# Moving the decode of the second MoE's weights out of the x2 stages, with three result buffers and two raw weight buffers

## The chip, the cores and the metric

The kernel runs on one core of a Trainium2 chip. Its metric is the device time of one execution in microseconds (us), and the median of several executions is what is compared. The engines are named as the profile names them: PE (TensorE, with its weight loads as PEld), DVE (VectorE), ACT (ScalarE), POOL (GpSimd), SP (the queue that issues nearly all DMAs here).

## The reference

An attention with packed queries, a first MoE and a second MoE, one after the other. There are 8 batches, 8 heads, 576 positions, 64 columns a head, so 4608 tokens of 512 columns.

```python
p_packed = sm_attn(p, k, v)            # 32 packed queries for each head
x = sm_attn(q, p_packed, p_packed)     # 576 queries on 32 keys
x = x.transpose(0, 2, 1, 3).reshape(4608, 512)
y = maximum(maximum(x @ w1, x @ w2), x @ w3)   # 512 -> 768
x2 = y @ w_out                                 # 768 -> 512
h = x2 @ w_in                                  # 512 -> 2048
P = a[0] + a[1]*h + a[2]*h**2 + a[3]*h**3
Q = 1 + abs(b[0])*abs(h) + abs(b[1])*h**2
out = (P / (Q + 1e-6)) @ w_out2                # 2048 -> 512
```

All weights of the two MoEs arrive as 64-bit floats.

## The kernel before

**Arithmetic.** Every fp32 product is made of three matmuls of a high and a low part (`mm3`, lines 61 to 63). A weight in 64 bits has to be taken apart into these parts on the core first. `decode` (lines 76 to 95) does it for one piece of 128 rows: it loads the raw words (`w_raw`, 64 bits a number), and then runs five instructions on DVE (L76, L80 or L78, L85, L87, L92 or one of them less), two on ACT (L81, L82) and one on POOL (L95). All DVE instructions of it read or write `w_raw`.

**Stages.** The first MoE goes over four pairs of batches (`bp` 0 to 3). For each pair there is a stretch of y stages: six blocks `f` of the 768 columns, two batches and three weights `w1`, `w2`, `w3` each, so 36 turns of 12 matmuls, and behind each turn the function `between` puts other work in. The maximum over the three weights is kept in a tile `hm` of the pool `hx`. The attention is folded into the weights: `m_stage` (L313) multiplies a tile of weights `wt` by the packed attention into the matrix `m` that y uses, twelve times a pair. Behind the y stages come eight x2 stages (`x2_stage`, two batches by four blocks of 128 columns), which multiply the maxima by `w_out`, bring the result from PSUM into a tile `hm` again (L477, on ACT or DVE) and store it to memory (L478). Between the x2 stages of pairs 0 to 2 stands the second softmax of the next pair (`s2_stage`, lines 275 to 293), whose transposed result also takes a tile `hm` (L293). PSUM has two banks pairs, `psy`, for y, x2 and this softmax.

**The two feeds.** `feed` decodes the first MoE's 12 pieces of w1 to w3 and 4 pieces of w_out during pair 0 (pieces of 768 columns). `feed2` decodes the second MoE's 32 pieces (512 columns) during pairs 1 to 3. One `feed2.step()` finishes a piece (L85, L87, L92 and POOL's L95 write it into a tile `wt`), stores it to memory (L235), issues the load of a further raw piece (L100) and starts the next piece (L76, L80, ACT's L81 and L82). The first step only starts one. Before the change the steps stand behind turns 1, 5, ..., 33 of the y stages of pairs 1 and 2, behind four x2 stages of pair 1 and three of pair 2, and behind turns 1, 5, ..., 29 of pair 3: 13 + 12 + 8 = 33 steps.

**Rings.** `wt` is a ring of four tiles that the decoded pieces share with the `w1` to `w3` tiles, which are read back from memory for each pair (`again`, L216). A `wt` tile that `m_stage` has used is free for the next that waits. `w_raw` is a ring of three, and `feed` and `feed2` load that many pieces ahead. `hm` is a ring of two.

**What sets the order.** The program's order is not that of the queues. The framework simulates the program at build time and issues, of the instructions whose inputs and buffers are there, the one that stands earliest in the program; a buffer that comes free goes to the earliest of those that wait. So decoding can be pulled ahead of the turn where it is written, as far as the rings allow. On the chip each engine keeps the order found in that way and waits for what is late. The second MoE's matrix work (`h_mm`, `g_stage`, `o_mm`) begins when the last x2 stage is done and runs to the end.

Of the kernel before, what the change touches and what calls it, by code (L numbers as in the profile page):

```python
# [33 lines left out]
def attn_moe_moe2_kernel(  # L34
# [16 lines left out]
    def split(hi, lo, src, hi_eng="act", lo_eng="dve"):  # L51

        if hi_eng == "act":
            act.copy(hi, src)  # L54
        else:
            nc.vector.tensor_copy(hi, src)
        e = dve if lo_eng == "dve" else pool
        e.tensor_tensor(out=lo, in0=src, in1=hi.bitcast(F32), op=ALU.subtract)  # L58
# [108 lines left out]
    bstack, ctx2 = ExitStack(), ExitStack()  # L167
# [10 lines left out]
    rstack = ExitStack()  # L178
    wp = rstack.enter_context(tc.tile_pool(name="wp", bufs=1, side="right"))
    mp = [rstack.enter_context(tc.tile_pool(name=f"mp{x}", bufs=1, side="right")) for x in range(2)]  # L180
    hx = bstack.enter_context(tc.tile_pool(name="hx", bufs=2))


    wt_ready, NWT, NW = {}, 4, 12
# [16 lines left out]
        return tiles, w123[2 * f + g], keep, True  # L201

    used = itertools.count()
    NRAW = 3

    def next_wt():

# [16 lines left out]
    def w2_pieces():  # L224

        for i in range(32):
            box = []

            def tiles(box=box):
                box.append(wt_tile())  # L230
                hi, lo = (box[0][:, x] for x in range(2))
                return (hi.bitcast(I32) if wide else hi.bitcast(F32R)), lo.bitcast(F32R)

            def keep(box=box, i=i):
                nc.sync.dma_start(w2_scr[:, :, 512 * i : 512 * i + 512], box[0])  # L235

            yield tiles, w_2[i], keep, False

    def load_w2(tiles, o, n):

        for x in range(2):
            nc.sync.dma_start(tiles[:, x].bitcast(F32), w2_scr[:, x, 512 * o : 512 * (o + n)])
# [56 lines left out]
    def m_tiles(f):  # L299

        return [mp[f % 2].tile([128, 2, 2, 384], F32R, name=f"m{x}") for x in "hl"]

    def m_stage(bp, g, mt):

        ps = ps_t.tile([128, 2, 512], F32, name="pst")
        wt, n = next_wt()
        for b2 in range(2):
            for h in range(4):  # L310
                i, j = divmod(h, 2)
                l, c = slice(64 * j, 64 * j + 64), 32 * (h ^ b2)
                pe.matmul(ps[c : c + 32, b2, :384], lhsT=ppk[l, bp % 2, 2 * g + b2, 32 * h : 32 * h + 32],  # L313
                          rhs=wt[l, 384 * i : 384 * i + 384], start=True, stop=True)
        again(n)
        split(*(t[:, :, g, :] for t in mt), ps[:, :, :384])
# [130 lines left out]
    def y_stage(b2, f, m, a2, between, lo_eng):  # L447
        hm = hx.tile([128, 2, 288], F32, name="hm")
        mh, ml = m
        for w in range(3):  # L450
            ps = ps_y.tile([128, 2, 512], F32, name="psy")
            for half in range(2):
                for g in range(2):
                    ah, al = a2[g]
                    c = slice(288 * half, 288 * half + 288)
                    mm3(ps[:, half, :288], mh[:, g, 128 * w : 128 * w + 128], ml[:, g, 128 * w : 128 * w + 128],
                        ah[:, c], al[:, c], g == 0, g == 1)
            if w == 0:
              act.copy(hm, ps[:, :, :288])
            else:  # L460
              dve.tensor_tensor(out=hm, in0=ps[:, :, :288], in1=hm, op=ALU.max)  # L461
            between()
        hh = hp_pool.tile([128, S], F32R, name=f"hh{b2}{f}")
        hl = hp_pool.tile([128, S], F32R, name=f"hl{b2}{f}")
        split(hh, hl, hm.rearrange("p a b -> p (a b)"), lo_eng=lo_eng)
        return hh, hl
# [13 lines left out]
    def wi_at(f):  # L480

        if f < 1:
            return wi_0
        return wi_b[:, :, f - 1]
# [18 lines left out]
    ahead = Ahead(0)  # L503
    feed = Feed(wp, pieces, NRAW)
    for x in "P L0 L1 W0 R W1 L2 L3 R".split():
# [5 lines left out]
    pool.memset(cln[:, 1:2], -LN64)  # L511
    feed2 = None

    y_steps = {1: range(1, 36, 4), 2: range(1, 36, 4), 3: range(1, 32, 4)}
    windows = (), (0, 2, 4, 6), (1, 3, 5)
    for bp in range(NBP):
        turn = itertools.count()
        if bp == 1:
            feed2 = Feed(wp, w2_pieces(), NRAW, NRAW)
        if bp == NBP - 1:  # L520

            nc.sync.dma_start(av, a_in.partition_broadcast(128))
            nc.sync.dma_start(bv, b_in.partition_broadcast(128))
            dve.tensor_scalar(out=babs, in0=bv, scalar1=-1.0, scalar2=None, op0=ALU.mult)
            dve.tensor_tensor(out=babs, in0=babs, in1=bv, op=ALU.max)
        now = ahead
        a2, mt = ahead.a2, ahead.mt
        hs = [[None] * 6, [None] * 6]
        if bp + 1 < NBP:
            ahead = Ahead(bp + 1)  # L530
            for x in "P L0 W0 L1 W1".split():
                ahead.do(x)
            pack = ahead.steps(PACK)
        else:
            pack = iter(())
        for f in range(6):
            if f < 5:
                nmt = m_tiles(f + 1)

            def between(bp=bp, f=f, now=now):  # L540
                t = next(turn)
                if now.soft:
                    now.do("g")
                if f < 5 and t % 6 in (2, 4):
                    m_stage(bp, t % 6 // 2 - 1, nmt)
                if t >= 2:
                    next(pack, None)
                if bp == 0:
                    if t % 3 < 2 and t < 32:
                        feed.half_step()  # L550
                elif t in y_steps[bp]:
                    feed2.step()

            if bp == NBP - 1 and f == 2:
                load_w2(wi_at(0), 0, 1)
            for b2 in range(2):
                hs[b2][f] = y_stage(b2, f, [t[:, b2] for t in mt], a2[b2], between,
                                    "dve" if bp == 0 or (b2, f) == (1, 5) else "pool")
            mt = nmt
        if bp + 1 < NBP:  # L560
            assert not list(pack)
            gen = ahead.steps(SECOND)
            for m in range(4):
                for b2 in range(2):
                    x2_stage(2 * bp + b2, m, hs[b2])
                    next(gen, None)
                    if bp == 0:
                        feed.half_step()
                    if 2 * m + b2 in windows[bp]:
                        feed2.step()  # L570
            if bp == 0:
                assert not feed.raw and not feed.half
            next(gen, None)
            assert not ahead.soft
        else:
            assert not feed2.raw and not feed2.half
            rstack.close()
            NQA = 1
            wr = ctx.enter_context(tc.tile_pool(name="wr", bufs=1, side="right"))
            xpa = ctx.enter_context(tc.tile_pool(name="xpa", bufs=1, side="right"))  # L580
            wi_b = wr.tile([128, 2, 15, 512], F32R, name="wi_b")
            wq_a = wr.tile([128, 2, NQA, DM], F32R, name="wq_a")

            def wq_at(f):
                return wq_a[:, :, f] if f < NQA else wq_b[:, :, f - NQA]

            def load_x(blk, xp):
                xh = xp.tile([128, 4, 512], F32R, name="xh")
                xl = xp.tile([128, 4, 512], F32R, name="xl")
                for kc in range(4):  # L590
                    xr = xp.tile([128, 512], F32, name="xr", bufs=1)
                    nc.sync.dma_start(xr, x2_scr[:, kc, 512 * blk : 512 * blk + 512])
                    split(xh[:, kc, :], xl[:, kc, :], xr, lo_eng="pool" if blk > 1 else "dve")
                return xh, xl

            loads = [(wi_at(f), f) for f in range(1, 16)] + [(wq_at(f), 16 + f) for f in range(NQA)]
            per = -(-len(loads) // 8)
            for b2 in range(2):
                for m in range(4):
                    for _ in range(min(per, len(loads))):  # L600
                        tiles, o = loads.pop(0)
                        load_w2(tiles, o, 1)
                    if (b2, m) == (0, 2):
                        xc = load_x(0, xpa)
                    x2_stage(2 * bp + b2, m, hs[b2])
# [129 lines left out]
```

## Time and profile before

| | |
|---|---|
| time, median of 3 runs (lowest to highest) | 1390.62 us (1390.1 to 1392.14) |
| time of the profiled execution | 1393.72 us |
| its span, first to last instruction | 1391.8 us |
| mean granted clock of PE in it | 0.975 |
| PE busy | 1313.8 us, 94% of the span |
| DVE busy | 1051.1 us, 76% |
| ACT busy | 802.2 us, 58% |
| POOL busy | 242.7 us, 17% |

The time of an execution holds some 2 us outside the span. Busy shares are means over stages with different limits, so the stages are looked at one by one further on. A granted clock of 1 is 2.4 GHz, one of 0.5 is 1.2 GHz.

### The profile page before, as it was taken

How to read it: one execution, taken by the hardware profiler on the slowest of the kernel's cores; microseconds unless marked ns; L12 is line 12 of the kernel's file. 1: busy time of each engine (PE TensorE's matmuls, PEld its weight loads, DVE VectorE, ACT ScalarE, POOL GpSimd, SP SyncE). 2: the span in 40 equal slices, each digit the busy share in tenths (PEclk: the TensorE clock that was granted, in tenths of full speed). 3: DMA queues.
4: the chain of work that ended last, by engine and by line, in shares of the span. 5: the costliest groups of instructions: out<-in, count | busy, mean ns of one | idle time of the engine just before them, and what ended most of it. 6: DMA issues, size and time to landing. Idle time of an engine off the chain costs nothing.

```text
span 1391.8 us, 21572 instructions
## 1 busy us (share of the span) xinstructions
PE 1313.8 (94%) x8496; PEld 1091.5 (78%) x8496; DVE 1051.1 (76%) x1630; ACT 802.2 (58%) x1337; POOL 242.7 (17%) x230
## 2 busy tenths in 40 slices
PE   4479899998999899999999999999999999999998
PEld 1267788878878789978888888888888888888886
DVE  5877845767677765178888988888888888888887
ACT  3444523543443333176766867768677686776765
POOL 3542242425333533000100101001010010100000
PEclk9589899999999999999999999999999999999999
DMA  9945544677464721970100101001001010010000
GB/s 307 308 138 167 158 144 145 213 230 245 155 209 156 237 93 55 325 278 1 47 14 1 61 1 38 23 0 62 0 25 37 0 54 0 16 38 1 31 0 31
DMA packets 51557, 140.86 MB, mean 101 GB/s; under 512 B 5632, under 2 KB 5632, under 8 KB 50688
## 3 DMA queue, kind: packets, MB, share of 16 engines
q1 hardware_dynamic: 51168, 138.96, 30.0%
q8 instruction: 67, 1.10, 0.3%
q10 hardware_dynamic: 288, 0.52, 0.1%
q14 instruction: 34, 0.28, 0.1%
HBM read 99.09 MB, written 40.37 MB: 100 GB/s over the span
## 4 chain that ended last, share of the span: by engine, by line
PE 81%; DVE 5%; DMA 4%; ACT 2%; issue 1%; POOL 1%; SPq 0%; ACTq 0%; POOLq 0%; DVEq 0%
PE po L61 10%; PE po L62 9%; PE po L63 9%; PE psh L62 9%; PE psh L61 9%; PE psh L63 9%; PE psy L61 8%; PE psy L62 7%; PE psy L63 7%; PE pst L313 2%; DMA wi_b<-w_scr 1%; DMA w_raw<-in_w_dram 1%; DMA x_scr<-hm 1%; PE pst L378 1%; DVE wt L87 1%
## 5 line engine op out<-in xcount | busy, mean ns | idle before, releaser
L61 PE MATMUL po<-wq_b,gh 128*128 128x512 f32 x540 | 212.3, 393 | 0.8 <-ACT gh L54 0.8
L62 PE MATMUL po<-wq_b,gh 128*128 128x512 f32 x540 | 211.3, 391 | 0.0
L62 PE MATMUL psh<-xl,wi_b 128*128 128x512 f32 x540 | 211.0, 391 | 0.0
L63 PE MATMUL psh<-xh,wi_b 128*128 128x512 f32 x540 | 210.6, 390 | 0.0
L61 PE MATMUL psh<-xh,wi_b 128*128 128x512 f32 x540 | 210.6, 390 | 0.0
L634 ACT ACTIVATE hb<-psh,babs 128x512 f32<-128x512 f32 (+1 forms) x145 | 100.2, 691 | 188.8 <-PE psh L63 188.8
L61 PE MATMUL psy<-a2h,mh 128*128 128x288 f32 x576 | 181.6, 316 | 17.1 <-DVE hm L461 8.1
L63 PE MATMUL po<-wq_b,gl 128*128 128x512 f32 x540 | 181.7, 391 | 0.0
L637 DVE SCALAR_TENSOR_TENSOR hb<-h,babs,hb 128x512 f32<-128x512 f32 (+1 forms) x145 | 108.2, 746 | 97.1 <-ACT h L635 97.0
L62 PE MATMUL psy<-a2l,mh 128*128 128x288 f32 x576 | 172.7, 300 | 4.4 <-POOL a2l L58 4.4
L63 PE MATMUL psy<-a2h,ml 128*128 128x288 f32 x576 | 172.0, 299 | 0.0
L58 POOL TENSOR_TENSOR xl<-xr,xh 128x512 fp32r<-128x512 f32 x28 | 36.6, 1306 | 633.5 <-ACT xh L54 633.5
L61 PEld LDWEIGHTS psy<-a2h,mh 128*128 128x128 f32 x576 | 110.3, 192 | 44.4 <-issue 12.9
L61 PE MATMUL psy<-hh,wo_h 128*128 128x288 f32 x384 | 117.2, 305 | 12.1 <-ACT hm L477 11.7
L63 PEld LDWEIGHTS po<-wq_b,gl 128*128 128x128 f32 x540 | 101.3, 188 | 24.0
L461 DVE TENSOR_TENSOR hm<-psy,hm 128x576 f32<-128x576 f32 x96 | 72.4, 754 | 63.2 <-PE psy L63 60.3
L61 PEld LDWEIGHTS po<-wq_b,gh 128*128 128x128 f32 x540 | 101.4, 188 | 22.9 <-ACT gh L54 1.2
L62 PEld LDWEIGHTS po<-wq_b,gh 128*128 128x128 f32 x540 | 101.4, 188 | 22.4
L61 PEld LDWEIGHTS psh<-xh,wi_b 128*128 128x128 f32 x540 | 101.4, 188 | 22.1
L62 PEld LDWEIGHTS psh<-xl,wi_b 128*128 128x128 f32 x540 | 101.4, 188 | 21.7
L63 PEld LDWEIGHTS psh<-xh,wi_b 128*128 128x128 f32 x540 | 101.4, 188 | 21.7
L62 PE MATMUL psy<-hl,wo_h 128*128 128x288 f32 x384 | 115.5, 301 | 0.0
(104 smaller groups left out, 2816.0 us busy)
## 6 DMA issues: line engine op xcount, KB each, us to landing
w_raw<-in_w_dram SPq DMA_DIRECT2D x32, 512.0 KB, 4.7
w_scr<-wt SPq DMA_DIRECT2D x32, 512.0 KB, 3.3
wt<-w_scr SPq DMA_DIRECT2D x36, 384.0 KB, 4.0
kt<-in_k_dram SPq DMA_DIRECT2D x16, 576.0 KB, 6.2
vraw<-in_v_dram SPq DMA_DIRECT2D x16, 576.0 KB, 6.5
w_raw<-in_w_dram SPq DMA_DIRECT2D x12, 768.0 KB, 12.0
kt<-in_q_dram SPq DMA_DIRECT2D x16, 576.0 KB, 6.2
x_scr<-hm SPq DMA_DIRECT2D x32, 288.0 KB, 3.3
```

Source lines behind the costliest of these rows:

```text
L58: e.tensor_tensor(out=lo, in0=src, in1=hi.bitcast(F32), op=ALU.subtract)
L61: pe.matmul(out_ap, lhsT=lh, rhs=rh, start=first, stop=False)
L62: pe.matmul(out_ap, lhsT=lh, rhs=rl, start=False, stop=False)
L63: pe.matmul(out_ap, lhsT=ll, rhs=rh, start=False, stop=last)
L87: dve.scalar_tensor_tensor(out=hib, in0=hw, scalar=-0x80000000, in1=t, op0=ALU.bitwise_and, op1=ALU.bitwise_or)
L313: pe.matmul(ps[c : c + 32, b2, :384], lhsT=ppk[l, bp % 2, 2 * g + b2, 32 * h : 32 * h + 32], rhs=wt[l, 384 * i : 384 * i + 384], start=Tru ...
L378: pe.matmul(pv[32 * h : 32 * h + 32, :64], lhsT=at[:, 3 * i + cp, o : o + 32], rhs=vt[:, h, c, :], start=c == 0, stop=c == VC - 1)
L461: dve.tensor_tensor(out=hm, in0=ps[:, :, :288], in1=hm, op=ALU.max)
L634: act.activation(hb, h, AF.Abs, scale=babs[:, 0:1])
L637: dve.scalar_tensor_tensor(out=hb, in0=h2, scalar=babs[:, 1:2], in1=hb, op0=ALU.mult, op1=ALU.add)
```

## The change

Four edits. The pool `hx` gets three buffers instead of two. `NRAW`, the number of `w_raw` buffers and of raw pieces loaded ahead, becomes two instead of three; it holds for both feeds, so for the start of the kernel too. The steps of `feed2` between the x2 stages are gone, and the y stages have more: behind turns 1, 4, ..., 34 in pairs 1 and 2, and behind 1, 5, ..., 33 in pair 3. The count is 12 + 12 + 9 = 33 again.

```diff
-    hx = bstack.enter_context(tc.tile_pool(name="hx", bufs=2))
+    hx = bstack.enter_context(tc.tile_pool(name="hx", bufs=3))
...
-    NRAW = 3
+    NRAW = 2
...
-    y_steps = {1: range(1, 36, 4), 2: range(1, 36, 4), 3: range(1, 32, 4)}
-    windows = (), (0, 2, 4, 6), (1, 3, 5)
+    y_steps = {1: range(1, 36, 3), 2: range(1, 36, 3), 3: range(1, 36, 4)}
...
                     if bp == 0:
                         feed.half_step()
-                    if 2 * m + b2 in windows[bp]:
-                        feed2.step()
```

## Rows read from the trace of the kernel before

**Rows 1.** The page's chain that ended last, share of the span by engine.
```profile
PE 81%; DVE 5%; DMA 4%; ACT 2%; issue 1%; POOL 1%; SPq 0%; ACTq 0%; POOLq 0%; DVEq 0%
```

**Rows 2.** Windows: length, PE, PEld, DVE, ACT, POOL busy (instructions), clock, DMA share, GB/s.
```profile
0.00:54.00 54.00, 25.72 (x381) 12.29 (x381) 31.87 (x63) 20.96 (x40) 19.95 (x34) 0.81 0.98 316
54.00:172.20 118.20, 94.36 (x919) 74.29 (x919) 95.67 (x136) 57.27 (x93) 38.98 (x36) 0.86 0.53 170
172.20:215.90 43.70, 43.30 (x381) 39.86 (x377) 18.91 (x33) 11.21 (x18) 14.92 (x12) 1.00 0.38 130
215.90:298.70 82.80, 80.51 (x892) 66.92 (x890) 53.76 (x93) 38.25 (x71) 29.79 (x34) 1.00 0.60 188
298.70:350.50 51.80, 46.39 (x379) 42.91 (x373) 37.92 (x64) 18.59 (x30) 24.77 (x18) 0.93 0.75 255
350.50:434.00 83.50, 80.51 (x890) 66.89 (x888) 54.81 (x93) 38.18 (x71) 29.51 (x34) 1.00 0.50 163
434.00:487.60 53.60, 47.27 (x411) 42.81 (x405) 41.95 (x69) 20.44 (x32) 25.89 (x19) 0.94 0.72 237
487.60:554.40 66.80, 65.21 (x529) 58.76 (x528) 38.29 (x53) 24.58 (x38) 22.31 (x16) 1.00 0.21 72
554.40:592.80 38.40, 38.38 (x290) 38.15 (x288) 5.73 (x8) 7.52 (x13) 0.00 (x0) 1.00 0.90 314
594.90:1391.80 796.90, 792.10 (x3456) 648.67 (x3456) 670.86 (x1019) 564.59 (x934) 36.56 (x28) 1.00 0.09 32
```

**Rows 3.** Waits in 298.7:350.5: total us, times, longest.
```profile
PE psy L61 <- ACT hm L477: 5.4, 3, 2.4
```

**Rows 4.** Waits in 434:487.6.
```profile
PE psy L61 <- ACT hm L477: 6.3, 2, 5.3
```

**Rows 5.** Timeline around one such wait: start us, duration us, instruction [idle before, releaser].
```profile
320.07 1.60 POOL L283 TENSOR_TENSOR e<-e,mx 128x576 f32<-128x576 f32 x1
...
320.58 1.38 DVE L80 TENSOR_SCALAR dec_r<-w_raw 128x512 int32<-128x512 int32 x1
...
321.99 0.63 ACT L82 ACTIVATE dec_r<-dec_r 128x512 f32<-128x512 int32 x1 [3.39 <-DVE dec_r L80]
...
322.52 0.62 ACT L477 COPY hm<-psy 128x576 f32<-128x576 f32 x1
```

**Rows 6.** Windows of instructions on w_raw: length, DVE, POOL busy (instructions), clock, DMA, GB/s.
```profile
54.00:172.20 118.20, 46.26 (x49) 7.85 (x4) 0.86 0.53 170
172.20:215.90 43.70, 0.00 (x0) 0.00 (x0) 1.00 0.38 130
215.90:298.70 82.80, 20.07 (x35) 9.65 (x7) 1.00 0.60 188
298.70:350.50 51.80, 22.66 (x31) 7.85 (x6) 0.93 0.75 255
350.50:434.00 83.50, 20.97 (x35) 9.39 (x7) 1.00 0.50 163
434.00:487.60 53.60, 26.01 (x36) 9.16 (x7) 0.94 0.72 237
487.60:554.40 66.80, 13.65 (x21) 6.63 (x5) 1.00 0.21 72
```

**Rows 7.** Tile view of w_raw: landing of its loads, in 215.9:298.7, then in 0:54.
```profile
DMA to landing us min/median/max: 4.1/4.3/7.4
...
DMA to landing us min/median/max: 11.3/13.6/17.3
```

**Rows 8.** Timeline, the start: POOL finishes pieces 4 and 5, PE uses 4 and 5.
```profile
39.20 1.81 POOL L95 TENSOR_TENSOR wt<-wt,dec_t 128x768 f32<-128x768 f32 x1
...
47.47 1.81 POOL L95 TENSOR_TENSOR wt<-wt,dec_t 128x768 f32<-128x768 f32 x1 [1.82 <-issue]
...
60.12 1.54 PE L313 MATMUL pst<-wt,ppk 64*32 64x384 f32 x16 [4.70 <-DVE ml L58]
...
86.66 1.53 PE L313 MATMUL pst<-wt,ppk 64*32 64x384 f32 x16
```

## The prediction, made before the changed kernel was built or run

> **What bounds the kernel now.** I read the chain that ended last first: 81% of it is PE, and no other engine has more than 5% [rows 1]. So time is to be found where PE waits or runs at a lower clock, and the page's mean shares don't say where that is. Next I cut the span by stage with the view of windows [rows 2]. The last row is the second MoE: 796.9 us long, PE busy for 792.1. The change doesn't touch it. The stretches before it are the start (to 54.0), and then y and x2 by turns for the four pairs of batches.
>
> The three x2 stretches of pairs 0, 1 and 2 hold the same matmuls for x2 and the same second softmax of the next pair, and they last 43.7, 51.8 and 53.6 us. In the first, PE is busy for 43.30 of 43.7 at full clock, so 43.7 is what PE needs. The two others are 8.1 and 9.9 us longer, with PE busy 5.4 and 6.3 us less than their length and the clock at 0.93 and 0.94. What differs is seen in the same view with the instructions on `w_raw` alone [rows 6]: no decoding at all falls into the first, and 22.66 and 26.01 us of DVE's time into the other two. DVE is busy for 37.9 and 42.0 us there, against 18.9.
>
> The waits name the way from DVE to PE. In both stretches PE waits for ACT's eviction L477, 5.4 and 6.3 us in all, which is the whole of its idle time [rows 3, 4]. The timeline shows why the eviction is late [rows 5]: on ACT it stands behind L82, half a decode, which had waited 3.39 us for DVE's L80, and L80 took 1.38 us while POOL worked beside it. PE has two `psy` buffers, so a late eviction stops it. The y stretches of pairs 1 and 2 are another regime: PE busy for 80.51 of 82.8 and 83.5 us, DVE free for 29 us in each.
>
> **What the change removes and moves.** The seven steps between x2 stages go into y. But a piece isn't decoded where its step stands: it needs a `wt` tile, which in y only an `m_stage` gives free, and a freed tile goes to the earliest in the program that waits, a piece or a read-back (`again`). From rows 6 the pieces now fall so: five DVE instructions each, so 7 in y of pair 1 (35/5), 6.2 in its x2 (31/5), 7 and 7.2 in pair 2, 4 to 5 in pair 3's y. I went through the ring by hand with the new steps. With a step at turns 4, 7, 10, ... a piece stands ahead of the read-backs at nearly every one of the eight `m_stage`s that run inside y, so about 9 pieces land in y instead of 7. In pair 1, x2 then keeps 2 to 3 of 6.2 pieces (the last two of its own and the first of pair 2). In pair 2 the next pair's steps at turns 1, 5 and 9 stand ahead of read-backs too and are pulled into x2, so 5 of 7.2 stay. Pair 3's y gets one more.
>
> *x2, pair 1.* The excess of 8.1 us is 1.3 us for each of 6.2 pieces. Left with 2.5 pieces it would be 3.3 us in proportion, and nothing if DVE's slack takes them: without decoding DVE needs 37.92 - 22.66 = 15.3 us here, and 2.5 pieces at 22.66/6.2 = 3.65 us add 9.1, in 43.7 us. I take 1.5 left, a gain of 6.6. *x2, pair 2.* 9.9 us for 7.2 pieces; with 5 left it is 6.9 in proportion, and at best 0. Since 5 are most of 7.2, I stay nearer to proportion: 4.0 left, a gain of 5.9. Together -12.5, bounds -18.0 (both at 43.7) and -7.8 (both in proportion, 4.8 + 3.0).
>
> *y.* Five more pieces, at 20.07/7 = 2.87 us of DVE each, against 29 us of DVE that are free in each of the two long stretches. What hides them is that slack; without it each would cost what it costs in x2, 1.3 to 1.4 us, so the bounds are 0 and +6.9. I take +1.5, because DVE is in order and the maximum L461, which frees `psy`, stands behind whatever is put in.
>
> *Two raw buffers in y.* A buffer is held from its load's issue to POOL's end: 4.3 us to landing [rows 7], 2.87 DVE, two ACT instructions like the 0.63 of rows 5, 9.65/7 = 1.38 POOL, together 9.8 us. Two buffers give a piece every 4.9 us, and three turns take 82.8/36*3 = 6.9 us, so there are 2.0 us to spare. At the worst landing, 7.4, it is 6.5 us and still inside. Behind a late load L76 waits on DVE, and behind it L461. Bounds 0 and +6 (one of four of the 24 pieces late by 1 us), taken +0.5.
>
> *Two raw buffers at the start.* Here a load takes 13.6 us [rows 7], since DMA is busy at 0.98 [rows 2]. A piece of 768 columns has four DVE instructions on `w_raw`, 46.26/49*4 = 3.8 us. A buffer is held for 13.6 + 3.8 + 1.3 (ACT) + 1.8 (POOL, rows 8) = 20.5 us, so a piece every 10.2 us instead of 6.8: the pieces lag by about one. Pieces 4 and 5 are ready at 41 and 49 now and used at 60 and 87 [rows 8], so a lag of 8 to 13 us reaches nobody. But about one piece's DVE work (3.8 us) moves from before 54 into the first y turns, where DVE is busy for 95.67 of 118.2 and PE idle for 24. Bounds -3 (less decoding in DVE's way while the softmax of pair 0 is waited for) and +6 (the piece's work in full and some clock); taken +1.
>
> The skill has a line on buffers: the Trainium skill, "Trainium Kernel Development and Optimization", Best Practices, advises double-buffering so that DMA and compute overlap, and by it the cut to two would cost nothing anywhere. The trace agrees in y (4.9 us against 6.9) and not at the start (10.2 against the 8.3 us between two pieces in rows 8); by the page the sum would be 1.5 us lower than mine.
>
> *The third `hm` buffer.* Nothing on PE's path waits for `hm` in rows 3 and 4: the evictions there wait in ACT's line, not for the tile. Taken 0, bounds -2 (the store of an x2 result holds its tile while loads crowd the DMA) and 0.
>
> *Sum.* -12.5 + 1.5 + 0.5 + 1.0 = -9.5 us. The profiled execution took 1393.72 us, so it would be 1384.2; the median of the runs is 3.1 us lower, so 1390.62 - 9.5 = **1381.1 us**.
>
> **The rivals.**
> *All of the excess.* Both x2 stretches fall to 43.7 and y hides its pieces: -18.0, and -1 at the start where less is decoded early: 1371.6. For it: DVE needs only 15 to 19 us of an x2 stretch without decoding [rows 2, 6]. Against: 5 pieces remain in pair 2 by the ring. The Trainium skill, "Perfetto Trace Analysis", Optimization Strategy, says that a kernel with several regimes may gain from interleaving them; this change does that, and by that rule alone this rival is the forecast.
> *The ring decides, not the step.* If read-backs still win the freed tiles in y, x2 keeps its 6 and 7 pieces less one each: -2.7, and +1 at the start: 1389. For it: the steps written in y now already slip into x2, 13 pieces there for 7 steps written there. Against: at 8 `m_stage`s and 12 steps a piece stands in line nearly every time.
> *Slower: DVE and POOL don't run beside each other.* Rows 5 show L80 at 1.38 us with POOL at work; in y DVE's 53.76 and POOL's 29.79 us make 83.6 of 82.8. If they exclude each other fully, y has no slack and five pieces cost 5 * (2.87 + 1.38) = 21.2 us: 1390.6 - 12.5 + 21.2 = 1399. It decides from the point where the cost of a moved piece passes 2.5 us (12.5/5). Against: PE's idle time in y is only 2.3 us at that sum, and a piece costs DVE less there (2.87) than in x2 (3.65). The Trainium skill, "SBUF — State Buffer", Who interferes with whom, says that POOL and those DVE instructions that read two SBUF inputs or run in a two-port mode block each other for a whole instruction; by it only part of DVE's work is excluded, which is between this rival and my sum.
>
> **How the numbers follow.** My sum 0.53 (own range 1376 to 1387), all of the excess 0.20, the ring 0.15, slower 0.12. A change within 0.2%, 2.8 us, can't be told from none, so the bounds are 1387.8 and 1393.4. Faster: 0.53 + 0.20 + 0.02 of the ring = 0.75; same 0.13; slower 0.12. The likeliest is 1381; the range leaves out a third of the first rival (below 1371) and most of the slower one (above 1391): 1371 to 1391.
>
> **What the changed profile would show.** Right: instructions on `w_raw` on DVE about 10 and 18 us in the x2 stretches of pairs 1 and 2 and about 26 in each of their y stretches; those x2 stretches at about 45 and 48 us, PE's wait for L477 under 2 and 4 us, the clock at 1.00 and 0.97; y within 2 us of 82.8 and 83.5; the second MoE unchanged. The start right: first y matmul within 3 us of 54 and pair 0's y within 3 us of 118. Wrong: more than 6 pieces in an x2 stretch (the ring); y longer by 5 us or more, with L461 late behind decode instructions or L76 waiting for `w_raw`; or pair 0's end moved by more than 6 us, since the order there is found anew and its waits are the least predictable of the kernel.

## The result, and the profile after

The changed kernel takes 1408.84 us (median of 4 runs, 1405.61 to 1413.01) against 1390.73 for the kernel before beside it: a ratio of 1.013, 95% interval 1.0115 to 1.0145. It is slower by 18 us where the prediction said 1381, and outside the range of 1371 to 1391.

The windows by stage of the changed kernel, columns as in [rows 2]: start, y and x2 of pairs 0 to 2, y of pair 3, and the second MoE.

```profile
0.00:57.60 57.60, 24.43 (x380) 11.37 (x380) 32.30 (x65) 22.46 (x42) 19.87 (x35) 0.83 0.96 311
57.60:174.80 117.20, 96.23 (x944) 75.38 (x940) 91.28 (x135) 56.73 (x92) 37.56 (x35) 0.89 0.51 166
174.80:217.30 42.50, 41.96 (x360) 39.12 (x353) 18.53 (x33) 10.26 (x17) 14.92 (x12) 1.00 0.34 115
217.30:314.30 97.00, 88.70 (x906) 70.54 (x904) 67.61 (x107) 40.34 (x75) 33.49 (x37) 0.96 0.61 194
314.30:360.70 46.40, 43.97 (x365) 40.83 (x358) 24.93 (x45) 14.55 (x23) 17.63 (x14) 0.96 0.56 192
360.70:456.30 95.60, 87.25 (x906) 68.89 (x905) 66.69 (x108) 40.55 (x75) 33.15 (x37) 0.98 0.54 176
456.30:507.90 51.60, 46.60 (x393) 42.81 (x390) 30.35 (x55) 17.24 (x27) 21.34 (x16) 0.93 0.53 182
507.90:575.30 67.40, 65.95 (x529) 58.93 (x528) 41.32 (x58) 25.50 (x40) 23.41 (x17) 1.00 0.28 95
...
614.70:1411.20 796.50, 791.76 (x3456) 648.62 (x3456) 671.33 (x1020) 563.02 (x934) 36.53 (x28) 1.00 0.10 32
```

Beside [rows 2], x2 gives nearly what it should in pair 1 (51.8 to 46.4) and a third of it in pair 2 (53.6 to 51.6); up to the end of the first x2 the kernel is 1.4 us later (217.3 for 215.9); the second MoE is as it was. The whole loss stands in two rows: y of pair 1 went from 82.8 to 97.0 and y of pair 2 from 83.5 to 95.6, 26.3 us together. Neither PE nor DVE is full there: PE waits for 8.3 us of each, and DVE is busy for 67.6 of 97.0.

The same view with the instructions on `w_raw` alone, from y of pair 1 on, answers to [rows 6] (columns as there).

```profile
217.30:314.30 97.00, 35.31 (x49) 13.18 (x10) 0.96 0.61 194
314.30:360.70 46.40, 7.14 (x12) 2.61 (x2) 0.96 0.56 192
360.70:456.30 95.60, 34.46 (x49) 13.01 (x10) 0.98 0.54 176
456.30:507.90 51.60, 13.62 (x22) 5.26 (x4) 0.93 0.53 182
```

At five instructions a piece these are ten pieces in each y instead of seven, 2.4 in x2 of pair 1 and 4.4 in pair 2: the count in the prediction (9, then 2 to 3, and 5) was nearly right. But a DVE instruction on `w_raw` in y took 20.07/35 = 0.57 us before and takes 35.31/49 = 0.72 now. The waits in y of pair 1 (total us, times, longest), in the kernel before and then in the changed one, show two that DVE had hardly or not at all there before, and PE behind them:

```profile
DVE hm L461 <- PE psy L63: 13.9, 9, 3.6
...
PEld psy L61 <- DVE hm L461: 1.4, 2, 0.7
...
DVE dec_t L76 <- DMA w_raw<-in_w_dram: 1.2, 1, 1.2
```

```profile
DVE dec_t L76 <- DMA w_raw<-in_w_dram: 5.9, 5, 2.1
DVE hm L461 <- PE psy L63: 5.1, 5, 2.4
...
PEld psy L61 <- DVE hm L461: 4.4, 6, 1.2
...
DVE wt L87 <- DMA w_scr<-wt: 3.1, 3, 1.5
```

L76 is the first instruction of a piece and waits for its load; L87 is the first that writes the piece's `wt` tile, and waits until the store of the piece that had the tile before has been read out. L461, which frees `psy`, stands behind them on DVE: it waits 5.1 us for PE, where it waited 13.9 before, and PE's weight loads wait 4.4 us for it instead of 1.4. The chain that ended last, cut to this y (by line, the costliest first; the view ends its lines there), in the kernel before and then in the changed one:

```profile
by line: PE psy L61 25.0%; PE psy L63 21.3%; PE psy L62 21.2%; PE pst L313 7.9%; PE pst L378 5.7%; DMA w_raw<-in_w_dram 5.0%; PE pst L367 3.8%; PE psy L337 2.3%; ACT e L349 1.9%; DVE hm L461 1.8%; DVE mx L342 1.8%; issue 1.7%; DVE wt L87 1.
```

```profile
by line: DMA w_scr<-wt 16.0%; DMA w_raw<-in_w_dram 8.9%; issue 8.3%; POOL wt L95 8.3%; PE psy L61 7.6%; PE psy L62 6.6%; PE psy L63 6.6%; DMA kt<-in_q_dram 6.3%; DVE wt L87 4.7%; DVE w_raw L92 3.4%; DVE hm L461 2.9%; DVE dec_t L76 2.9%; PE 
```

Before, y's own matmuls (L61 to L63) were 67.5% of it, and now they are 20.8%; the stores of decoded pieces, their loads and POOL's L95 have come in. For the whole program, the page's chain answers to [rows 1]:

```profile
PE 73%; DMA 7%; DVE 6%; POOL 2%; issue 2%; ACT 2%; SPq 0%; POOLq 0%; ACTq 0%; DVEq 0%
```

### The profile page after: what moved, and what is told of

The parts are those of the page before. It is cut to its first block, busy times and chain, and to the rows that moved or that the text cites. A ratio compares the mean times of both kernels' runs of the same rounds, so it can differ in the third digit from the quotient of the medians.

```text
span 1411.2 us, 21551 instructions
## 1 busy us (share of the span) xinstructions
PE 1325.3 (94%) x8496; PEld 1094.7 (78%) x8496; DVE 1050.9 (74%) x1630; ACT 798.9 (57%) x1337; POOL 237.9 (17%) x230
## 4 chain that ended last, share of the span: by engine, by line
PE 73%; DMA 7%; DVE 6%; POOL 2%; issue 2%; ACT 2%; SPq 0%; POOLq 0%; ACTq 0%; DVEq 0%
PE po L61 9%; PE po L62 9%; PE po L63 9%; PE psh L62 9%; PE psh L61 9%; PE psh L63 9%; PE psy L61 6%; PE psy L62 5%; PE psy L63 5%; DMA w_raw<-in_w_dram 3%; DMA w_scr<-wt 3%; POOL wt L95 1%; PE pst L313 1%; DVE wt L87 1%; DVE dec_t L76 1%
## 5 line engine op out<-in xcount | busy, mean ns | idle before, releaser
L61 PE MATMUL po<-wq_b,gh 128*128 128x512 f32 x540 | 212.2, 393 | 0.8 <-ACT gh L54 0.8
L63 PE MATMUL psh<-xh,wi_b 128*128 128x512 f32 x540 | 210.6, 390 | 0.0
L61 PE MATMUL psh<-xh,wi_b 128*128 128x512 f32 x540 | 210.4, 390 | 0.0
L61 PE MATMUL psy<-a2h,mh 128*128 128x288 f32 x576 | 184.0, 320 | 16.3 <-DVE hm L461 7.2
L63 PE MATMUL po<-wq_b,gl 128*128 128x512 f32 x540 | 182.6, 391 | 0.0
L634 DVE SCALAR_TENSOR_TENSOR hb<-h,babs,hb 128x512 f32<-128x512 f32 (+1 forms) x145 | 108.3, 747 | 96.3 <-ACT h L632 96.2
L63 PE MATMUL psy<-a2h,ml 128*128 128x288 f32 x576 | 173.6, 301 | 0.0
L61 PEld LDWEIGHTS psy<-a2h,mh 128*128 128x128 f32 x576 | 111.5, 194 | 51.5 <-DVE hm L461 15.3
L61 PE MATMUL psy<-hh,wo_h 128*128 128x288 f32 x384 | 116.8, 304 | 8.0 <-ACT hm L477 7.2
L63 PEld LDWEIGHTS po<-wq_b,gl 128*128 128x128 f32 x540 | 101.3, 188 | 23.9
L61 PEld LDWEIGHTS po<-wq_b,gh 128*128 128x128 f32 x540 | 101.4, 188 | 22.9 <-ACT gh L54 1.2
L61 PEld LDWEIGHTS psh<-xh,wi_b 128*128 128x128 f32 x540 | 101.4, 188 | 22.0
L63 PEld LDWEIGHTS psh<-xh,wi_b 128*128 128x128 f32 x540 | 101.4, 188 | 21.7
L62 PEld LDWEIGHTS psy<-a2l,mh 128*128 128x128 f32 x576 | 112.0, 194 | 4.7 <-POOL a2l L58 4.7
```

The lines of the kernel that those rows point to most:

```text
L61: pe.matmul(out_ap, lhsT=lh, rhs=rh, start=first, stop=False)
L62: pe.matmul(out_ap, lhsT=lh, rhs=rl, start=False, stop=False)
L63: pe.matmul(out_ap, lhsT=ll, rhs=rh, start=False, stop=last)
L634: dve.scalar_tensor_tensor(out=hb, in0=h2, scalar=babs[:, 1:2], in1=hb, op0=ALU.mult, op1=ALU.add)
```

## The experiments

All were timed in turns with the kernel before, whose median was 1390.4 to 1391.0 us in each series. The stage columns are from each run's trace, x2 from its first to its last matmul and y what lies between. A trace is of one execution; that of e12 was 6.9 us longer than its median, the others lie within 4.2 us of theirs.

| run | edit to which kernel | median us | ratio (95%) | y 1 | x2 1 | y 2 | x2 2 |
|---|---|---|---|---|---|---|---|
| before | | 1390.7 | | 82.8 | 51.8 | 83.6 | 53.6 |
| after | | 1408.8 | 1.0130 (1.0115-1.0145) | 96.9 | 46.5 | 95.4 | 51.7 |
| e1 | before, two raw buffers | 1406.0 | 1.0117 (1.0095-1.0139) | 90.3 | 53.5 | 90.3 | 50.3 |
| e2 | before, new steps | 1403.4 | 1.0092 (1.0077-1.0107) | 94.2 | 47.9 | 89.5 | 51.2 |
| e3 | before, both | 1406.9 | 1.0115 (1.0098-1.0132) | 97.5 | 45.5 | 96.4 | 51.1 |
| e4 | e1, third `hm` | 1402.7 | 1.0097 (1.0064-1.0130) | 91.7 | 53.4 | 90.9 | 50.3 |
| e5 | after, fifth `wt` | 1412.3 | 1.0150 (1.0118-1.0182) | 96.7 | 46.5 | 96.5 | 48.7 |
| e6 | e1, later start | 1404.5 | 1.0104 (1.0087-1.0121) | 91.9 | 51.2 | 90.7 | 50.3 |
| e7 | before, two loaded ahead | 1390.5 | 0.9997 (0.9987-1.0006) | 83.5 | 52.1 | 82.7 | 53.5 |
| e8 | before, steps to pair 3 | 1389.4 | 0.9991 (0.9982-1.0001) | 83.5 | 47.9 | 83.5 | 53.2 |
| e9 | e1 for the second MoE alone | 1403.8 | 1.0122 (1.0079-1.0164) | 90.5 | 50.3 | 92.1 | 52.1 |
| e10 | e1, no loads | 1399.9 | 1.0066 (1.0044-1.0087) | 88.5 | 47.9 | 88.4 | 54.8 |
| f1 | before, no loads | 1383.6 | 0.9951 (0.9935-0.9967) | 82.7 | 48.2 | 82.7 | 53.0 |
| e11 | after, no loads | 1398.1 | 1.0041 (1.0021-1.0060) | 90.8 | 46.5 | 90.8 | 51.8 |
| e12 | e2, POOL stores | 1396.4 | 1.0040 (1.0023-1.0057) | 89.6 | 50.4 | 87.5 | 50.7 |
| f4 | before, POOL stores | 1397.7 | 1.0047 (1.0031-1.0064) | 86.8 | 49.8 | 86.6 | 55.3 |
| f2 | after, POOL stores | 1412.8 | 1.0160 (1.0138-1.0182) | 96.3 | 48.2 | 97.3 | 51.6 |
| f3 | e11, POOL stores | 1395.5 | 1.0032 (1.0015-1.0049) | 92.4 | 45.8 | 90.3 | 50.4 |
| g1 | e1, `m_stage` whole | 1402.8 | 1.0091 (1.0075-1.0106) | 90.7 | 48.9 | 92.9 | 53.1 |
| g2 | after, `m_stage` whole | 1402.0 | 1.0077 (1.0060-1.0094) | 94.1 | 45.8 | 93.1 | 51.6 |

**Which edit costs.** The change was taken apart: `NRAW = 2` alone (e1), the steps alone (e2), both without the third `hm` buffer (e3), and the two buffer edits without the steps (e4). A third `hm` buffer beside three raw buffers doesn't fit in the space left and wasn't tried.

> Two raw buffers alone, steps and the two result buffers as before. If the steps behind every third turn are what lengthens y (theory A: they crowd the ring of wt tiles, and DVE, which keeps its order, waits for stores and loads), this costs little: 1390 to 1394 us, y of pairs 1 and 2 at 81 to 84 us. If the missing third raw buffer is what lengthens y (theory B: DVE waits in order for raw pieces that are loaded too late), y grows here too and the time is 1396 to 1408. The start alone may move it by 3 us either way.

> The steps moved into y alone, three raw buffers and two result buffers. Theory A: y of pairs 1 and 2 still grows by 10 to 14 us each, the time is 1402 to 1410. Theory B: y stays within 3 us of before and the x2 stretches get shorter by 7 us together, so 1381 to 1386.

> Steps and two raw buffers, two result buffers: the change without the third hm buffer. Theories A and B both give 1406 to 1411. If the third hm buffer is what does the harm (theory C: it lets the order found at build time change in y), 1381 to 1390.

> The two buffer edits without the moved steps. Theory A: 1389 to 1394. Theory B: 1396 to 1408, as with two raw buffers alone. Theory C: above 1400, and more than 3 us above two raw buffers alone.

Raw buffers alone cost 15.6 us, the steps alone 13.0, both 16.5: each is enough, and they don't add. The third `hm` buffer makes no difference clear of the scatter (e4 against e1, after against e3: the intervals overlap). The windows of e1 and of e2 over y and x2 of pair 1 (columns as in [rows 2]) show different stretches:

```profile
215.40:305.70 90.30, 85.17 (x905) 68.02 (x903) 58.73 (x95) 37.83 (x71) 30.67 (x35) 1.00 0.54 178
305.70:359.20 53.50, 47.01 (x358) 43.78 (x358) 36.11 (x61) 18.62 (x30) 22.17 (x18) 0.90 0.70 238
```

```profile
214.10:308.30 94.20, 82.69 (x890) 68.69 (x889) 61.94 (x103) 40.19 (x75) 31.81 (x36) 0.96 0.59 188
308.30:356.20 47.90, 44.81 (x379) 41.33 (x373) 26.32 (x49) 14.86 (x24) 18.76 (x15) 0.96 0.60 210
```

With the steps, PE's work is little more than before (82.7 for 80.5 us) and it waits for 11.5 us; with two raw buffers its busy time itself is 4.7 us longer at full clock.

**The steps and their stores.** The longest wait of e2 in its timeline (start, duration, instruction, idle before and releaser):

```profile
280.38 0.57 SPq L235 DMA_DIRECT2D w_scr<-wt  x1
...
288.32 0.69 DVE L87 SCALAR_TENSOR_TENSOR wt<-w_raw,dec_t 128x512 int32<-128x512 int32 x1 [5.44 <-DMA w_scr<-wt]
...
289.96 0.72 ACT L81 ACTIVATE dec_t<-dec_t,reb 128x512 int32<-128x512 int32 x1 [5.68 <-DVE dec_t L76]
290.59 0.62 ACT L459 COPY hm<-psy 128x576 f32<-128x576 f32 x1
...
291.26 0.61 PE L61 MATMUL psy<-a2h,mh 128*128 128x288 f32 x1 [4.88 <-ACT hm L459]
291.39 0.75 DVE L461 TENSOR_TENSOR hm<-psy,hm 128x576 f32<-128x576 f32 x1
```

The store left at 280.4 and L87 of the next piece in that tile stood on DVE until 288.3; PE had nothing to do for 4.9 us. What released it was ACT's copy L459, which frees a bank of `psy`. On ACT, L459 stood behind L81, which had waited 5.68 us for L76, and L76 stood behind L87 on DVE. It is the kind of path by which the prediction explained x2's excess [rows 5], now in y. In all, L87 waited 8.7 us for stores in this stretch. A fifth `wt` tile (`NWT = 5`, e5) and stores issued by POOL instead of SP (e12, with its control f4 and, on the whole change, f2) are to take that away.

```
-                nc.sync.dma_start(w2_scr[:, :, 512 * i : 512 * i + 512], box[0])
+                pool.dma_start(w2_scr[:, :, 512 * i : 512 * i + 512], box[0])
```

> The whole change with a fifth wt tile. Theory A (a piece takes over the wt tile whose last content is still being stored, so that DVE, in order, waits for the store, with L461 behind it): the y stretches of pairs 1 and 2 shrink from 97.0 and 95.6 by some 6 us each, the waits of L87 for the store of wt go, and the time is about 1396 us. Theory B (two raw buffers: L76 waits on DVE for a late load) sees that wait left as it is: 1404 to 1409. If both halves are real and don't add, the time lies near that of the raw buffers alone, 1404 to 1406.

> The new steps alone with three raw buffers; the store of a decoded piece is issued by POOL right behind the instruction that completes it, not by SP's queue in the order of all loads. Theory A (L87 waits in DVE's order for a store that SP issued late or that landed behind other loads, 8.7 us in pair 1's y): those waits go, PE's gap of 4.9 us at 286 goes, y of pair 1 falls from 92.7 to about 85 and the time to 1392 to 1397. Rival (more pieces in y cost by DVE's time alone): y stays at 88 to 93, 1400 to 1405.

> The kernel before with the stores of the decoded pieces issued by POOL. Its waits of L87 for a store are 1.1 us in all in x2 of pair 1: within 2 us of before, 1388 to 1392. Rival: POOL's issue costs POOL time between its own instructions and the pieces are done later, 1393 to 1398.

> The whole change with the stores of the decoded pieces issued by POOL. If the waits of L87 for stores add to those for loads: 1400 to 1404 us, y at 91 to 94. If a wait taken away here only lengthens the next one (DVE waits for the load instead): 1405 to 1409, y at 94 to 97.

A fifth tile changes nothing: on the whole change, in y of pair 1, L87 still waits 3.1 us for stores. It was not run on the steps alone. POOL's stores cost the kernel before 7.0 us (f4), as the rival named there had it: POOL is busy for 34.6 us of y of pair 1 instead of 29.8. On the steps the same edit wins 7.0 us (e12 against e2), so about half of their 13.0 us goes with how the stores are issued. e12 has no wait of L87 for a store left in y of pair 1, but L76 waits 6.8 us for loads there, and y came to 89.6 us where 85 was expected. e12 lies 1.3 us below f4 (the intervals overlap): beside POOL's stores the new steps cost nothing more. That doesn't show that the stores are all of it, since two losses of this kernel needn't add, as the two edits didn't. On the whole change POOL's stores give nothing (f2).

**The raw buffers and their loads.** In e1, L76 waits 5.6 us for its loads in y of pair 1. e6 puts the start of a piece two turns later, e7 loads two ahead with three buffers, e9 keeps the third buffer for the start and pair 0. In e10, f1, e11 and f3 a finished piece hands its raw tile on without a new load: they leave out 30 of the 32 loads (f1, with three buffers, 29). f3 has POOL's stores besides.

```
+                elif t in y_steps[bp]: feed2.finish()          # e6
+                elif t - 2 in y_steps[bp]: feed2.start()
...
+            feed2 = Feed(wp, w2_pieces(), 3, 2)                # e7
...
+                old = self.old.pop(0) if self.old else load_raw(self.pl, piece[1], self.bufs)   # e10, f1, e11, f3
+                self.raw.append((old, piece))
```

> Two raw buffers alone, with the old steps, but in y the start of a piece stands two turns behind the end of the one before it instead of right behind it, which gives each load 4.6 us more. Theory B1 (a buffer is held over a whole step between start and finish, so the next load comes too late for the place that L76 has in DVE's order): the waits of L76 in y go, the y stretches come back from 89 to 82 to 84 us, and the time is 1390 to 1395. Rival B2 (fewer buffers cost in another way, by the order of the DMA queue or in the start): the y stretches stay at 88 to 90 and the time at 1403 to 1408.

> The kernel before with its three raw buffers, but only two pieces are loaded ahead, so that each load is issued a step later, as with two buffers, without having to wait for POOL to end with the buffer. B1 in its narrow form (the wait for POOL's end and the step together make the load late): between the two, 1394 to 1399. If the distance of the load from its use is all: as with two raw buffers, 1403 to 1408. If the number of buffers is all: as before, 1389 to 1392.

> Two raw buffers for the second MoE's pieces only; the pieces of the start and of pair 0 keep three (a third tile of its own that the second MoE's pieces don't use). Theory B (two raw buffers cost where the second MoE's pieces are decoded, in y and x2 of pairs 1 and 2): as with two buffers everywhere, 1402 to 1408 us. Rival (the loss is made by the order found for the start and pair 0, which shifts the tiles of all later rings): 1389 to 1393.

> Two raw buffers alone, and of the second MoE's pieces only the first two are loaded: every later piece decodes the tile that the piece two before it left, with the same instructions, so the kernel leaves out 30 loads of 512 KB. B as a wait (L76 stands in DVE's order where the load was expected and waits for it, with L461 behind it): the waits of L76 are gone, the y stretches are back at 82 to 84 us, the time is 1384 to 1392. Rival C (the other order that two buffers bring, with DVE's instructions stretched by POOL's beside them): the y stretches keep at least 5 of their 7 us more, 1398 to 1406.

> The whole change, with all but the first two loads of the second MoE's pieces left out as in the run before. If the waits of L76 for its loads (6.0 and 5.9 us in the two long y stretches) carry the loss: y at 84 to 88, time 1386 to 1396. If it is carried by DVE's work itself, which grew by three pieces a stretch and by 7 us of longer instructions beside POOL's, and by the waits of L87 for stores: y stays at 92 to 97, 1400 to 1409.

> The control for the runs without loads: the kernel before, three raw buffers, with all but the first three loads of the second MoE's pieces left out. If a load costs only where an instruction waits for it, nothing changes in y (no wait of L76 there but one of 1.2 us): 1388 to 1391 us, and what the runs without loads won came from the waits. If 30 loads less speed up everything that shares the DMA: 1380 to 1386, and the raw buffers' loss is then an order and not a wait.

> The whole change with both removed: the second MoE's loads left out but for two, and the stores issued by POOL. What is left over the kernel before is DVE's own work (three more pieces in each long y, with the longer instructions beside POOL) and the changed order, less what x2 gains. If the waits for DMA are all of the loss: 1381 to 1388, as the prediction's sum. If DVE's work carries a part: y at 86 to 90, 1390 to 1398.

e6 and e7 do nothing, because the order found is the old one: e6's is that of e1 on every engine, and e7's that of the kernel before but for two DMA issues that changed places; in all four traces the first load of a piece in y of pair 1 leaves 13.6 us after its start. So where a start or a load is written doesn't matter here, and what a later start or load would cost these two runs can't say. (That the same order took 1404.5 us in e6 and 1406.0 in e1 shows how far two series differ.) e9 shows that the loss belongs to the second MoE's pieces. e10 looked like a success for the waits, 6 us won, until its control: without loads the kernel before wins 7.1 us as well (f1), only 0.9 of it in the two long y. Two raw buffers cost 16.3 us without any load to wait for (1399.9 against 1383.6) and 15.6 with. The windows over the long y of pair 1, of f1 and then of e10 (pair 2 has 82.7 and 88.4 us):

```profile
213.10:295.80 82.70, 80.49 (x891) 66.91 (x889) 54.78 (x93) 38.20 (x71) 29.73 (x34) 1.00 0.46 150
```

```profile
211.50:300.00 88.50, 84.56 (x905) 67.95 (x903) 58.42 (x96) 38.69 (x71) 29.86 (x35) 1.00 0.45 144
```

So 5.8 of the 7.5 us in y of pair 1 are there without waits for loads, at full clock, and 4.1 of them are time in which PE is busy. The theory that L76's waits carry the loss falls: they are at most the 1.7 us that e1 has over e10. The control isn't perfect, since leaving loads out changes the order too (on DVE e10 and e1 differ in 246 of 1635 places). For the whole change the same comparison leaves 14.6 us (e11 over f1) of 18.1. f3 came to 1395.5, where its expectation put DVE's own work and the order, with y at 92.4 and 90.3, longer than the 86 to 90 named; the kernel before with both edits was not run.

**The order.** What two raw buffers still change is the order found at build time. PE's program at its 1470th matmul, an `m_stage` in y of pair 1, in the kernel before and in e1:

```
before   L313 MATMUL pst<-wt,ppk x8
e1       L313 MATMUL pst<-wt,ppk x6     (the other two stand behind matmuls of y)
```

In the whole program the `m_stage`s stand in 46 uninterrupted runs before, 7 of them shorter than a whole one, and in 59 in e1, 25 of them shorter. The steps alone (e2) break up none more: 46 runs, 6 of them shorter. The chain of e1 shows what a part costs (start, duration, how many records; a matmul of L313 has two):

```profile
247.82 0.79 PE pst L313 x12
...
250.40 0.77 PE pst L313 x4
...
258.68 0.81 PE pst L313 x16
```

Four records take as long as sixteen. Windows of L313 alone over y of pair 1 (PE and PEld busy, clock, DMA, GB/s), for the kernel before, e1, after, f1 and e10 (L313 is L318 in the last two):

```profile
215.90:298.70 82.80, 9.35 (x174) 2.10 (x174) 1.00 0.60 188
```

```profile
215.40:305.70 90.30, 13.44 (x188) 2.78 (x188) 1.00 0.54 178
```

```profile
217.30:314.30 97.00, 14.11 (x188) 2.87 (x188) 0.96 0.61 194
```

```profile
213.10:295.80 82.70, 9.31 (x174) 2.10 (x174) 1.00 0.46 150
```

```profile
211.50:300.00 88.50, 13.25 (x188) 2.91 (x188) 1.00 0.45 144
```

One `m_stage` more falls into y (out of the x2 behind it), and L313 has 4.1 us more in e1 and 4.8 after. Without loads it has 3.9 more too, which is two thirds of the 5.8 us between e10 and f1; the added `m_stage`, whole, would be some 0.8 of it. g1 and g2 queue the other seven matmuls right behind the first:

```
+                if not (b2 or h):
+                    whole.enter_context(tc.issue_after(mm.ins))
+                    whole.enter_context(tc.high_priority())
```

> Two raw buffers alone, with the eight matmuls of every m_stage kept together in PE's order (the seven others are queued right behind the first). Theory D: with two raw buffers the order found at build time breaks some of the m_stages of the long y stretches into six and two matmuls with y's own between them, and a part takes PE about as long as a whole (L313 fills 12.6 us of PE's time there instead of 8.7 with one m_stage more, and each return to y costs L61 0.2 us more). Then L313 comes down to 9.5 us, the two y stretches lose 4 us each and the time is 1393 to 1399. Rival (the order costs elsewhere, or by waits): y keeps 88 us or more, 1402 to 1408.

> The whole change with every m_stage kept together in the same way. Theory D: L313 fills 13.3 us of PE's time in the changed y stretches and comes down to 9.5, with 1 us less of L61; some 5 us less in each of the two, and the rest of the loss (PE's gaps, DVE's longer line and its waits) stays: 1396 to 1401. If the broken m_stages were all of it: 1381 to 1390. If they cost nothing: 1405 to 1412.

The same window, L313 being L314 there, and the whole y of pair 1, both of g1, then its waits:

```profile
214.10:304.80 90.70, 10.52 (x192) 2.22 (x192) 1.00 0.58 187
...
214.10:304.80 90.70, 82.82 (x909) 67.38 (x908) 59.93 (x97) 38.28 (x72) 30.23 (x35) 1.00 0.58 187
```

```profile
DVE dec_t L76 <- DMA w_raw<-in_w_dram: 5.2, 5, 2.2
PEld psy L61 <- DVE hm L466: 4.7, 6, 1.9
```

L313 came down by 2.9 us, about as expected, and y didn't: PE's work fell by 2.4 us and its idle time rose from 5.1 to 7.9, much of it for DVE's maximum (L461, here L466; PE's weight loads wait 4.7 us for it, against 0.7 in e1). In pair 2 y is no shorter either (92.9 for 90.3). The time fell by 3.2 us for the raw buffers, none of it in y, and with overlapping intervals; for the whole change it fell by 6.9, clear of the scatter, with 2.8 and 2.3 in the two y. So with the loads left in, PE waits for DVE instead of working on the parts. Without the waits (e10) L313 is most of what y loses; without the breaks (g1) the waits take their place. Whole `m_stage`s without loads were not run, nor on the kernel before; the first would show whether the two together are all of it.

**Another distribution.** e8 keeps three raw buffers and the old density in the long y, leaves two steps in each x2, and puts eleven into pair 3.

```
-    y_steps = {1: range(1, 36, 4), 2: range(1, 36, 4), 3: range(1, 32, 4)}
-    windows = (), (0, 2, 4, 6), (1, 3, 5)
+    y_steps = {1: range(1, 36, 4), 2: range(1, 36, 4), 3: range(1, 34, 3)}
+    windows = (), (2, 6), (1, 5)
```

> Another distribution with three raw buffers: y of pairs 1 and 2 keeps its step at every fourth turn, x2 has two steps each instead of four and three, and y of pair 3 has eleven steps instead of eight (every third turn). Theory A (it is the density in the long y stretches that costs): those keep 82 to 84 us, the x2 stretches lose 1 to 2 pieces and 2 to 3 us each, pair 3's y hides its pieces: 1384 to 1388. Rival (a step at every third turn crowds wherever it stands, since pair 3 has two turns' worth of DVE less to spare): pair 3's y grows by 5 us or more and the time is 1390 to 1396.

x2 of pairs 1 and 2 lost 3.9 and 0.4 us, and pair 3's y grew from 66.8 to 70.3: the whole is 1.6 us faster, and the interval (0.9982 to 1.0001) includes no change. No version that computes the whole beat the kernel before by more than that.

## Why the prediction was wrong

**Where the kernel's time is, and the ring: mostly right.** The pieces moved as counted, and x2 got shorter where they left. But x2's excess isn't DVE's decoding alone: f1 has the same 31 decode instructions in x2 of pair 1 and takes 48.2 us there instead of 51.8, at a clock of 1.00 instead of 0.93, with nothing but loads left out. *x2, pair 1* was sized at -6.6 and measured -5.4. *x2, pair 2* was sized at -5.9 and gave -2.0, outside its bound: 4.4 pieces left 51.6 us, so the excess is no price per piece; in the chain that ended last, 8.1 us of that stretch are stores of decoded pieces. The start (+1 taken, +1.4 at the end of the first x2) can't be told from none: the same point lies between 209.7 and 220.8 us in the runs with two raw buffers, and between 212.7 and 215.9 in those that start with three. The first y matmul was 3.6 us later and not within 3.

**"y" failed.** It said that DVE's 29 free us hide five pieces (+1.5 taken), at worst for what a piece costs in x2, +6.9 in all. The steps alone cost 11.4 and 5.9 us in the two y for four more pieces. Free time on an engine that works in order was taken for cover. A `wt` tile passes from one piece straight to the next, so L87 stands behind the store of the former, up to 5.4 us. Behind L87 stand, on DVE, the maximum L461 and, by way of L76 and ACT's L81, the copy L459; both free `psy`. PE idles for only 2.3 us of such a y; the prediction took that for a sign that nothing is lost there, and it is as much a sign that PE had nothing to spare.

**"Two raw buffers in y" failed, by more.** It was taken at +0.5, bounds 0 and +6; alone it cost 15.6. Its working was wrong: a buffer was to be held for 9.8 us. In e1 one was loaded from 229.0 on and POOL was done with it at 245.7, 16.7 us, since a piece is started at one step and finished only when a tile is there; the others of that y were held for 14.0 to 29.9. In the changed kernel, with its denser steps, they were held for 14.9 to 20.0 us in y of pair 1. Two buffers thus gave a piece every 7.5 to 10.0 us and not every 4.9, where three turns were to take 6.9. But what follows from that is mainly not the wait that the step named: e10 and f1 show that most of the loss is there without loads. What is left after them is the order on the engines, the same instructions found in another order when a buffer comes free later at build time. Without loads, 3.9 of the 5.8 us in a long y are the `m_stage`s; with loads, keeping them whole gives y nothing back. How the rest divides among the other exchanges on DVE and PE stays open. The Trainium skill, "Trainium Kernel Development and Optimization", Best Practices, advises two buffers for overlap; here two instead of three cost 1.2%, and lost overlap of load and work, the waits of L76, was at most 1.7 of the 7.5 us that e1 lost in y of pair 1.

**The rivals.** "All of the excess" fell with x2 of pair 2 and with y, "the ring" by the count of pieces. The slower one had the right sign (1399) and a part of the mechanism: DVE's instructions on `w_raw` grew by 26% in y. In e1's timeline one stands beside POOL:

```profile
274.80 1.98 POOL L58 TENSOR_TENSOR hl<-hm,hh 128x576 fp32r<-128x576 f32 x1 [2.92 <-ACT hh L54]
...
275.53 1.53 DVE L92 TENSOR_SCALAR w_raw<-wt 128x512 int32<-128x512 int32 x1
```

The same L92 took 0.43 us where POOL was idle; here it ended 0.3 us after POOL's. By the Trainium skill, "SBUF — State Buffer", Who interferes with whom, an instruction of either engine can hold the other up for its whole length; this row agrees. The rival's point of decision, 2.5 us for a moved piece, was passed: 26.3 us for six pieces, 4.4 each (with the steps alone 17.3 us for four, 4.3 each). But no run took POOL's work away from beside DVE's, so what it costs isn't known, and that the time came out within 10 us of this rival's 1399 is in part luck: the waits for stores and the changed order, which carry what the runs show, are not in it.

Why the two losses don't add is argued, not shown: both spend the same margin of the long y, and once DVE's order sets its pace, a second disturbance finds PE waiting already.

## What to carry to other kernels

The free time of an in-order engine is no cover by itself: ask what stands behind the inserted instruction, which tile it takes over, and which transfer must be done with that tile. Where the order is found at build time, a smaller ring can cost more than its waits, because what stands behind it is ordered anew; a loss is then not explained by the waits that the profile lists, and it takes a control that removes them from both kernels to see it (without f1 the loads would have been the story). A stage in which PE idles for 2 of 83 us was here the place to leave alone, not the one to fill.

## What the runs showed of the hardware

The granted clock fell after one long wait. Windows of 4 us in e2 around the gap of 4.9 us (columns as in [rows 2]):

```profile
285.30:289.30 4.00, 1.09 (x9) 0.81 (x7) 0.94 (x2) 0.00 (x0) 0.00 (x0) 0.90 0.79 309
289.30:293.30 4.00, 2.04 (x8) 2.04 (x9) 3.22 (x6) 2.56 (x4) 1.41 (x1) 0.50 0.28 103
293.30:297.30 4.00, 4.00 (x45) 3.74 (x44) 0.76 (x1) 1.31 (x2) 1.21 (x1) 0.75 0.83 262
```

PE was busy for 1.09 of 4 us, and was granted the lower of its two levels, 1.2 GHz, in the next 4 us and half of the 4 after that. In e1, four of the records of L313 took 0.77 us, where sixteen took 0.81. Stores moved from SP's queue to POOL's cost the kernel before 7.0 us (f4). Without 29 of its loads it was 7.1 us faster (f1), though its long y took 82.7 us each, for 82.8 and 83.5 with them.
